# A planned two-headed kernel with its 64 planner draws exchanged

## The chip, the cores and the metric

The kernel runs on one core of one Trainium2 chip. The metric is the device time of one execution in microseconds (us); less is better. Five engines of the core matter here. PE (TensorE) multiplies matrices, with PEld as its weight load; ACT (ScalarE) does the exponentials; DVE (VectorE) and POOL (GpSimd) do element-wise work; SP (SyncE) issues most DMAs. Each engine takes its instructions strictly in the order of the program, and engines wait for one another by semaphores.

## The reference: what is computed

Two independent computations share the launch, and their results stand side by side in the output (2048 x 1280, bf16).

The first (A) is a diagonal complex state-space layer over 2048 steps and 640 states; the second (B) is attention with 32 query heads of width 20 that share one key head and one value head:

```python
# A
Bu = einsum("bld,pd->blp", x, B_bar)
h[t] = Lam_bar * h[t-1] + Bu[t]                 # complex, t = 0..2047
y = 2 * einsum("blp,dp->bld", hseq, Cmat).real + x * Dskip
# B
q, k, v = x @ wq (32 heads of 20), x @ wk, x @ wv
p = softmax(q k^T * 20**-0.5)                   # 32 x 2048 x 2048
out = (p v) @ wo
```

The bulk is the softmax: 32 heads x 2048 x 2048 exponentials.

## The kernel before, in words

**Attention.** The 2048 queries are cut in 4 blocks of 512, the 32 heads in 8 groups of 4 heads, which makes 32 groups; the keys are cut in 16 pieces of 128. A unit is one head, one query block and one key piece, 128 x 512 scores, so a group has 64 units and the program 2048. The loop of `main` takes a group's units in small sets. A set is a fill: PE computes two or three units at once into a PSUM tile (`R0` with three banks, `R1` with two, in turn), and ACT then takes the whole tile in one exponential, `ex_op` at L1295, 128x1024 or 128x1536 wide, into the SBUF tile `P`. One further unit can ride along with a fill: a D unit. Its scores go to one of two spare PSUM banks, `B`, or to the third bank of `R0`, which the fill then leaves to it and is two wide. A D unit gets its exponential on DVE instead of ACT: `dx_op` at L1301 turns the scores to an integer whose bits read as a bf16 power of two, and `sh_op` at L1307 makes three shifted copies, in two instructions for each run of one to four neighbouring units. Four copies of one unit take four product matmuls where an ACT unit takes one. PE then multiplies the results with the values `VP` into the PSUM bank `PV` (rows `PV<-P` and `PV<-Pd`), four column strips at a time. When a group's 64 units are in, DVE copies `PV` out (`OTr`, L1343), and only then can the next group's products begin. Later, normalising (POOL, L1039) and projection (PE rows with `WO`) follow.

**State-space layer.** Per block of 512 steps and per 128 states: PE products with `BTre` and `BTim`, a DVE rotation (L929), PE sums, two DVE scans (L957), 24 small POOL instructions (L945) and, once five such steps are through, output products with `CGre` and `CGim`, copied out at L990. All of it is put between the attention's instructions, as are the query projections (rows `B<-xbT,wq` and `B<-xbT,wqd`).

**What sets the order.** Nothing is written out by hand. `Plan` keeps a clock for each engine from its own table of costs. In each turn `main` offers all work that could go next, with the start that `Plan` gives it and a bias, and takes the lowest; that appends the instruction to its engine's program. The biases are not fixed: the 2048 units are cut in 64 turns of 32, and at the start of a turn `vary` seeds a random generator with that turn's entry of `SEEDS` and draws about twenty settings: how much DVE work may be queued before a unit is no longer sent to it (`backlog`), how long background work may starve, the largest number of D units of a group (`quota`), the biases of fills, products, copies, shifts (`pvb`, `rawb`, `shb`), how many D units share a shift (`shift`), and the size of a random term in every bias (`noise`). The core of it:

```python
if self.units * self.TURNS // NU > turn:
    turn = self.units * self.TURNS // NU
    self.vary(self.SEEDS[min(turn, self.TURNS - 1)])
```

One more rule matters: where `Plan` sees PE idle for longer than a limit and its recent work sparse, it puts in zero products (rows `PV<-cs,VP`), which add nothing to `PV`.

Until the first fill (the setup: transposed loads, the key projection, tables of sines) the order comes from code and not from draws.

Of the kernel before, what the change touches and what calls it, by code (L numbers as in the profile page):

```python
# [254 lines left out]
class _Kernel:  # L255
# [18 lines left out]


    TURNS = 64
    SEEDS = (31, 1860, 2783, 3329, 4215, 5944, 6425, 7348, 8334, 9235, 10124, 11344, 12674, 13859, 14008,
# [4 lines left out]

    def __init__(self, nc, t):
        self.nc, self.t = nc, t
# [874 lines left out]
    def main(self):  # L1159
# [188 lines left out]
        while True:  # L1348
# [3 lines that stand above are left out]
            cand = []  # L1352
# [216 lines left out]
```

## Time and profile before

| | before |
|---|---|
| median of 3 runs | 760.76 us (759.37 to 761.68) |
| profiled execution, own time | 759.82 us |
| its span, first to last instruction | 758.1 us |
| ACT busy | 743.4 us (98%) |
| DVE busy | 699.6 us (92%) |
| PE busy | 697.1 us (92%) |
| POOL busy | 347.5 us (46%) |

A row of the table of groups has the line, the engine, the operation, out<-in with the tiles' names, the shape and the count; behind the bar the busy time in us and the mean duration of one in ns, then the engine's idle time ahead of them with what ended it. Instructions of one engine overlap at their ends, so a group's busy time divided by its count is less than the mean duration of one. The chain that ended last follows the work back from the last instruction to what released it. PEclk is the clock granted to PE, 1.00 being full.

### The profile page before, as it was taken

The page shows a single profiled execution, that of the slowest core. Times are in us where ns is not written, and L with a number is a line of the kernel's source. Part 1 is how long each engine was busy: PE and PEld are TensorE (multiplying, and loading weights), DVE is VectorE, ACT ScalarE, POOL GpSimd, SP SyncE. Part 2 cuts the span into 40 slices and gives each one's busy share as a digit, 9 for nine tenths or more (in the row PEclk, how much of TensorE's full clock was granted, in tenths as well). Part 3 has the DMA queues.
Part 4 walks back from the last instruction along what each step waited for, and adds up shares of the span by engine and source line. Part 5 has one row for each costly group of instructions (what it writes and reads, how often), then busy time and mean ns, then how long its engine had stood idle before and what let it go on. Part 6 is the DMA issues. An engine that isn't in the chain of part 4 may idle for free.

```text
span 758.1 us, 22782 instructions
## 1 busy us (share of the span) xinstructions
PE 697.1 (92%) x9725; PEld 226.4 (30%) x9725; DVE 699.6 (92%) x1084; ACT 743.4 (98%) x705; POOL 347.5 (46%) x708
## 2 busy tenths in 40 slices
PE   5899988888899999999999999899999999998788
PEld 2322222222224333222343232233322233332224
DVE  6699999999997899999999799999999989999976
ACT  8999999999999999999999999999999999999996
POOL 5701455479887001998304975730068880000040
PEclk9799999999999999999999999999999999998999
DMA  9486301000002100400001310020100210010011
GB/s 187 73 131 146 67 16 49 18 15 16 2 24 63 42 28 21 87 17 16 18 27 49 70 42 24 9 59 11 33 24 11 59 38 31 24 33 9 11 44 36
DMA packets 61202, 31.89 MB, mean 42 GB/s; under 512 B 41510, under 2 KB 61102, under 8 KB 61102
## 3 DMA queue, kind: packets, MB, share of 16 engines
q1 hardware_dynamic: 59606, 30.14, 16.8%
q8 instruction: 77, 1.26, 0.7%
q10 hardware_dynamic: 1496, 0.30, 0.2%
q14 instruction: 23, 0.19, 0.1%
HBM read 9.21 MB, written 12.69 MB: 29 GB/s over the span
## 4 chain that ended last, share of the span: by engine, by line
ACT 87%; PE 9%; DVE 3%; DMA 1%; issue 0%; ACTq 0%
ACT P L1295 85%; PE R L448 3%; PE B L448 3%; PE PV L448 3%; DVE Pd L1301 1%; DVE Pd L1307 1%; ACT cs L719 1%; DMA WO<-in_B_wk_dram 1%; ACT Pd L718 0%; ACT KT L565 0%; ACT L530 0%; DVE hh L957 0%; DVE tm L929 0%; ACT WO L507 0%; ACTq L421 0%
## 5 line engine op out<-in xcount | busy, mean ns | idle before, releaser
L1295 ACT ACTIVATE P<-R 128x1024 bf16<-128x1024 f32 (+2 forms) x672 | 724.2, 1333 | 4.3 <-PE B L448 2.2
L448 PE MATMUL R<-QT,KT 32*128 32x512 bf16 (+1 forms) x1674 | 264.8, 388 | 46.2 <-ACT P L1295 36.3
L1301 DVE TENSOR_SCALAR Pd<-B 128x512 int16<-128x512 f32 x374 | 251.8, 682 | 22.1 <-PE B L448 19.6
L448 PE MATMUL PV<-Pd,VP 128*32 128x512 bf16 x1820 | 262.6, 386 | 1.4 <-DVE OTr L1343 0.5
L448 PE MATMUL PV<-P,VP 128*32 128x512 bf16 x1593 | 261.5, 386 | 0.2
L1307 DVE TENSOR_SCALAR Pd<-Pd 128x1536 int16<-128x1536 int16 (+3 forms) x342 | 241.0, 711 | 2.5
L945 POOL TENSOR_TENSOR tm<-hh,cs 128x128 bf16<-128x128 f32 x320 | 164.5, 538 | 31.4 <-DVE hh L957 17.2
L448 PEld LDWEIGHTS R<-QT,KT 32*128 32x128 bf16 (+1 forms) x1674 | 66.1, 91 | 307.4 <-ACT P L1295 279.7
L448 PE MATMUL B<-QT,KT 32*128 32x512 bf16 x374 | 144.5, 386 | 0.0
L945 POOL TENSOR_TENSOR W<-tm 128x128 bf16<-128x128 bf16 x160 | 76.0, 498 | 124.9 <-PE B L448 121.0
L1039 POOL TENSOR_TENSOR OTd<-OTd,rwide 128x128 bf16<-128x128 bf16 x80 | 34.0, 452 | 108.8 <-DMA OTd<-o_rows 106.9
L448 PEld LDWEIGHTS PV<-Pd,VP 128*32 128x32 bf16 x1820 | 63.1, 95 | 61.3 <-issue 41.0
L448 PEld LDWEIGHTS PV<-P,VP 128*32 128x32 bf16 x1593 | 62.3, 95 | 45.3 <-issue 36.1
L1301 DVE TENSOR_SCALAR Pd<-R 128x512 int16<-128x512 f32 x81 | 55.2, 682 | 2.7 <-PE R L448 1.9
L929 DVE TENSOR_TENSOR tm<-B,cs 128x1024 bf16<-128x1024 f32 x40 | 48.6, 1215 | 3.2 <-PE B L448 3.0
L448 PE MATMUL B<-CGre,W 128*32 128x384 bf16 (+1 forms) x640 | 48.5, 304 | 0.5 <-DVE Pd L1301 0.5
L448 PE MATMUL B<-CGim,W 128*32 128x384 bf16 (+1 forms) x640 | 47.8, 299 | 0.0
L886 POOL TENSOR_SCALAR tm<-W,sc 128x128 f32<-128x128 bf16 x40 | 32.7, 831 | 31.7 <-DVE CGre L888 14.9
L961 POOL COPY hst<-hh 128x2 f32<-128x2 f32 x15 | 5.9, 394 | 72.4 <-DVE hh L957 72.2
L957 DVE TENSOR_TENSOR_SCAN hh<-sc,hini,B 128x512 f32<-128x512 f32 x30 | 37.6, 1268 | 0.6 <-PE B L448 0.3
L448 PEld LDWEIGHTS B<-QT,KT 32*128 32x128 bf16 x374 | 33.9, 91 | 0.7 <-issue 0.4
L448 PE MATMUL B<-xaT,BTre 128*32 128x512 bf16 x400 | 30.8, 383 | 0.7 <-DVE hh L957 0.3
(153 smaller groups left out, 470.2 us busy)
## 6 DMA issues: line engine op xcount, KB each, us to landing
o_rows<-OTr SPq DMA_DIRECT2D x32, 128.0 KB, 1.7
QT<-q_rows SPq DMA_DIRECT2D x30, 128.0 KB, 2.2
q_rows<-Qd SPq DMA_DIRECT2D x16, 160.0 KB, 2.9
OTd<-o_rows SPq DMA_DIRECT2D x16, 160.0 KB, 3.3
out_dram<-ystage SPq DMA_DIRECT2D x16, 160.0 KB, 1.8
out_dram<-ostage SPq DMA_DIRECT2D x12, 160.0 KB, 1.8
P<-in_B_wq_dram SPq DMA_DIRECT2D x1, 800.0 KB, 6.1
WO<-in_B_wo_dram SPq DMA_DIRECT2D x4, 200.0 KB, 3.2
```

The source lines that it names most:

```text
L448: ins = e.matmul(o() if callable(o) else o, lhsT=l, rhs=r, start=st, stop=sp, skip_group_check=True, **kw)
L719: act(lambda e, c=c, b=b: e.activation(K.cs[:, c, :, :].rearrange("p i n -> p (i n)"), K.tri[:, 4 * b + 2:4 * b + 4, :].rearrange("p r n - ...
L886: pool(lambda e, y=y, c=c, gy=gy, i=i: e.tensor_scalar(K.ctmp[:, i:i + 128], y[:, i:i + 128], sc[:, gy, c:c + 1], None, op0=ALU.mult), key ...
L929: dve(lambda e, k=k, h=h: e.tensor_tensor(K.tm[:, 2 * k:2 * k + 2, :], bass.AP(tensor=K.BB, offset=512 * int(h.key[1]), ap=[[512 * self.BA ...
L945: put(lambda e, c0=c0, end=end: e.tensor_tensor(out[:, c0:end], a[:, c0:end], b[:, c0:end], op), reads, [writes + h], n, gate=None if i el ...
L957: dve(lambda e, ri=ri, ini=ini, h=h: e.tensor_tensor_scan(K.hh[:, ri, :], dec, h.T[:, :], ini, ALU.mult, ALU.add), ["sc", None, "hini"], [ ...
L961: pool(lambda e: e.tensor_copy(K.hst[:, :, c:c + 1], K.hh[:, :, 511:512]), ["hh0", "hh1"], ["hst"], 40)
L1039: ops.append(Op("pool", lambda e, c=c, m=m: e.tensor_tensor(K.OTd[:, m, c], K.OTd[:, m, c], K.rwide[:, c], ALU.mult), rw + [f"OTe{dd}" for ...
L1295: return Op("act", lambda e: e.activation(dst, K.R[n % 2][:, 0:512 * size], ACT.Exp, scale=self.exp_scale), [f"R{n % 2}"] + ["R0c"] * (siz ...
L1301: return Op("dve", lambda e: e.tensor_scalar(K.Pd[:, 0, u, :], K.B[x][:, :], self.d_off, 0.0, op0=ALU.add, op1=ALU.max), [key], [f"Pd{u}_0 ...
L1307: return Op("dve", lambda e: e.tensor_scalar(K.Pd[:, i:i + n, a:b, :].rearrange("p s u n -> p s (u n)"), K.Pd[:, 0:n, a:b, :].rearrange("p ...
```

## The change

All 64 entries of `SEEDS` are other numbers. No other line differs:

```diff
     TURNS = 64
-    SEEDS = (31, 1860, 2783, 3329, 4215, 5944, 6425, 7348, 8334, 9235, 10124, 11344, 12674, 13859, 14008,
...
+    SEEDS = (19, 1987, 2263, 3089, 4041, 5474, 6444, 7290, 8492, 9186, 10683, 11194, 12742, 13024, 14829,
...
```

So every turn draws other settings and another noise, and from the first draw on each engine's program stands in another order. The setup is the same, instruction for instruction. Counted over the whole program, these numbers differ:

| instructions | before | after |
|---|---|---|
| ACT exponentials 128x1536 / 128x1024 / 128x512 | 250 / 421 / 1 | 225 / 454 / 0 |
| D units, from `B` / from `R` | 374 / 81 | 362 / 103 |
| shift runs of 1 / 2 / 3 / 4 units | 27 / 32 / 84 / 28 | 37 / 35 / 66 / 40 |
| products `PV<-P` / `PV<-Pd` | 1593 / 1820 | 1583 / 1860 |
| zero products `PV<-cs,VP` | 212 | 100 |

Everything else has the same count on every engine.

The first place is PE's program right after the setup. `R<-QT,KT` are a fill's scores, `B<-QT,KT` a D unit's; `B<-xbT,wq` is the query projection for the second group, `B<-Qabs,Mblk` its last step, `B<-xbT,wqd` belongs to later groups. Before:

```order
L448 MATMUL R<-QT,KT 128x512 x7
L448 MATMUL B<-xbT,wq 32x512 x20
L448 MATMUL R<-QT,KT 128x512 x5
L448 MATMUL PV<-P,VP 32x512 x4
L448 MATMUL B<-Qabs,Mblk 32x512 x4
L448 MATMUL B<-xbT,wqd 32x512 x20
```

After:

```order
L448 MATMUL R<-QT,KT 128x512 x7
L448 MATMUL PV<-P,VP 32x512 x8
L448 MATMUL R<-QT,KT 128x512 x3
L448 MATMUL PV<-P,VP 32x512 x4
L448 MATMUL R<-QT,KT 128x512 x2
L448 MATMUL PV<-P,VP 32x512 x8
L448 MATMUL R<-QT,KT 128x512 x3
L448 MATMUL B<-QT,KT 128x512
L448 MATMUL B<-xbT,wq 32x512 x20
L448 MATMUL R<-QT,KT 128x512 x2
```

The 20 projection matmuls stood ahead of the ninth fill and now stand behind the eleventh; products of the first fills, in batches of 4 to 8, have their place.

The second place is PE's program where it has least to do for the longest. Before, at fills 616 to 619 of 672, some nine tenths through:

```order
L448 MATMUL R<-QT,KT 128x512 x2
L448 MATMUL B<-QT,KT 128x512
L448 MATMUL PV<-P,VP 32x512
L448 MATMUL PV<-Pd,VP 32x512 x5
L448 MATMUL R<-QT,KT 128x512 x3
L448 MATMUL B<-QT,KT 128x512
L448 MATMUL PV<-P,VP 32x512
L448 MATMUL R<-QT,KT 128x512 x2
L448 MATMUL B<-QT,KT 128x512
L448 MATMUL R<-QT,KT 128x512 x3
L448 MATMUL B<-QT,KT 128x512
L448 MATMUL PV<-Pd,VP 32x512 x2
```

After, at fills 620 to 622 of 679, the same share of the way through, where PE again has little beside its fills:

```order
L448 MATMUL R<-QT,KT 128x512 x2
L448 MATMUL B<-QT,KT 128x512
L448 MATMUL PV<-Pd,VP 32x512 x4
L448 MATMUL R<-QT,KT 128x512 x3
L448 MATMUL PV<-Pd,VP 32x512 x2
L448 MATMUL PV<-P,VP 32x512
L448 MATMUL PV<-Pd,VP 32x512 x3
L448 MATMUL R<-QT,KT 128x512 x2
L448 MATMUL B<-QT,KT 128x512
```

Before, one product and then none stood between three fills in a row; now four and six stand between neighbouring fills.

8 rows, old and new, of the table SEEDS are left out of this document.

## The prediction

> **What bounds the kernel now.** I read the page's busy times and chain first, then ACT's timeline, because the chain names ACT.
>
> ```profile
> PE 697.1 (92%) x9725; PEld 226.4 (30%) x9725; DVE 699.6 (92%) x1084; ACT 743.4 (98%) x705; POOL 347.5 (46%) x708
> ...
> ACT 87%; PE 9%; DVE 3%; DMA 1%; issue 0%; ACTq 0%
> ...
> L1295 ACT ACTIVATE P<-R 128x1024 bf16<-128x1024 f32 (+2 forms) x672 | 724.2, 1333 | 4.3 <-PE B L448 2.2
> ```
>
> The 672 exponentials occupy ACT for 724.2 us and ACT stood idle ahead of them for only 4.3 us. ACT's timeline in order of time has a new row wherever it had to wait (in brackets, with what ended the wait):
>
> ```profile
> 20.88 9.17 ACT L1295 ACTIVATE P<-R 128x1536 bf16<-128x1536 f32 x8
> 31.30 2.37 ACT L1295 ACTIVATE P<-R 128x1536 bf16<-128x1536 f32 x2 [1.25 <-PE R L448]
> 34.27 196.33 ACT L1295 ACTIVATE P<-R 128x1536 bf16<-128x1536 f32 x178 [0.60 <-PE B L448]
> 230.93 115.15 ACT L1295 ACTIVATE P<-R 128x1536 bf16<-128x1536 f32 x108 [0.33 <-PE B L448]
> 346.46 345.61 ACT L1295 ACTIVATE P<-R 128x1536 bf16<-128x1536 f32 x326 [0.38 <-PE R L448]
> 693.08 2.53 ACT L1295 ACTIVATE P<-R 128x1536 bf16<-128x1536 f32 x2 [1.01 <-PE B L448]
> 695.87 53.49 ACT L1295 ACTIVATE P<-R 128x1536 bf16<-128x1536 f32 x48 [0.26 <-PE B L448]
> 753.52 0.70 ACT L1129 ACTIVATE W<-R 128x640 bf16<-128x640 f32 x1 [4.15 <-PE R L448]
> ```
>
> So the span is 20.88 us of setup, 724 us of exponentials, some 4 us of waits among them, and 758.1 - 749.36 = 8.7 us of tail. A wait on ACT costs its full length; on any other engine it costs nothing until ACT waits. DVE and PE are not idle partners, though:
>
> ```profile
> 40.00:740.00 700.00, 652.43 (x9132) 208.12 (x9133) 662.70 (x1010) 697.60 (x650) 321.34 (x643) 1.00 0.15 37
> 60.00:160.00 100.00, 86.32 (x1066) 24.12 (x1058) 97.51 (x155) 100.00 (x91) 44.84 (x61) 1.00 0.23 53
> 640.00:688.00 48.00, 45.61 (x715) 15.94 (x712) 47.27 (x80) 48.00 (x48) 0.00 (x0) 1.00 0.09 30
> ```
>
> These rows of busy time by stage (length, then PE, PEld, DVE, ACT, POOL, clock) show DVE at 662.70 / 700 = 94.7% in the middle of the program, and at 97.5% and 98.5% in stretches in which ACT still never waited.
>
> **The change, part by part.** *ACT's work.* 25 exponentials of 1536, and one of 512, become 33 of 1024, since ten more units go to DVE. Their price is the pace in an unbroken run, from two runs of the timeline split by form:
>
> ```profile
> L1295 ACT ACTIVATE P<-R 128x1536 bf16<-128x1536 f32 x76 | 124.3, 1635 | 0.7 <-PE B L448 0.6
> L1295 ACT ACTIVATE P<-R 128x1024 bf16<-128x1024 f32 x102 | 116.2, 1187 | 0.1
> ...
> L1295 ACT ACTIVATE P<-R 128x1024 bf16<-128x1024 f32 x218 | 227.9, 1177 | 0.0
> L1295 ACT ACTIVATE P<-R 128x1536 bf16<-128x1536 f32 x108 | 172.3, 1595 | 0.5 <-PE R L448 0.4
> ```
>
> With 76 b + 102 a = 196.33 and 108 b + 218 a = 345.61, a 1024 takes a = 0.912 us and a 1536 takes b = 1.360. Over the program 421 a + 250 b is 723.9, which with one of 512 meets the 724.2 of the page. The change is 33 x 0.912 - 25 x 1.360 - 0.46 (half a 1024) = **-4.4 us**. This is sure, being counts; what may be lost is the filling of ACT.
>
> *The start.* ACT's waits of 1.25 and 0.60 us come from here (the chain):
>
> ```profile
> 21.04 6.77 ACT P L1295 x6
> 27.85 0.61 PE R L448 x2
> 28.46 2.26 PE B L448 x20
> 30.72 1.08 PE R L448 x5
> 31.80 0.55 PE PV L448 x4
> 32.35 1.54 PE B L448 x24
> ```
>
> The ninth fill stands behind 20 projection matmuls, 2.26 us, and ACT, through with its eighth tile at 20.88 + 9.17 = 30.05, waits. After, eight products stand there, at 0.55 a batch of four about 1.1 us, so that fill begins near 29.6 and is there by 30.1. Two further fills (0.54 each) and 12 products (1.65) end near 32.9, with the ninth and tenth exponential over at about 32.4: 0.5 us lost. Then the 20 projections come; at the later pace (a batch of 24 in 1.54 us) about 1.2 us, and the fill behind them is there by 34.5 with ACT's eleventh over at about 34.2: 0.3 lost. At the earlier pace it would be 1.1 us more. The batch also feeds the second group's queries later, which delays D units, not ACT. Of 1.85 us 0.8 stay: **-1.0**, between -1.8 and +0.1.
>
> *The fall of the clock near 688 us.* Waits of 1.01 and 0.26 us come from this stretch (columns as above):
>
> ```profile
> 684.00:688.00 4.00, 2.82 (x29) 0.79 (x24) 4.00 (x7) 4.00 (x5) 0.00 (x0) 1.00 0.11 37
> 688.00:692.00 4.00, 3.50 (x31) 0.82 (x30) 3.97 (x6) 4.00 (x4) 0.00 (x0) 0.51 0.00 0
> 692.00:696.00 4.00, 4.00 (x43) 0.82 (x35) 2.49 (x5) 2.67 (x4) 0.00 (x0) 0.64 0.00 0
> ```
>
> PE had 2.82 us of work in 4, its clock was then 0.51, and work that had fitted no longer did. In PE's order this is the sparsest place of the program: fills 617 to 620 have 9 matmuls of other work among them (counted from the order). The next is 10, at fill 635, and there the timeline shows no wait. After the change the smallest such sum over four fills is 14 (at fills 470 and 620), and PE has fewer holes although zero products are halved. I take this fall as gone, **-1.3**; bounds -1.3 (no fall) and +1.3 (it recurs at two places).
>
> ```profile
> 686.69 0.39 PE L448 MATMUL R<-QT,KT 32*128 32x512 bf16 x3 [0.95 <-ACT P L1295]
> ```
>
> By the Trainium skill, page "TensorE: Matmul & The Clock Gate", section "What's actually happening", the clock drops after an idle window of some 3.4 us and stays up without such gaps. PE's longest wait in that stretch is the 0.95 us of the row above, so a window that is busy to two thirds suffices here; taken at its word the rule would see a fall in neither kernel, this term would be chance, and the sum 1.3 us higher.
>
> *DVE's work.* Ten more D units and another mix of shift runs:
>
> ```profile
> L1301 DVE TENSOR_SCALAR Pd<-B 128x512 int16<-128x512 f32 x374 | 251.8, 682 | 22.1 <-PE B L448 19.6
> L1307 DVE TENSOR_SCALAR Pd<-Pd 128x3072 int16<-128x3072 int16 x84 | 81.8, 974 | 0.5
> ...
> L1307 DVE TENSOR_SCALAR Pd<-Pd 128x1536 int16<-128x1536 int16 x84 | 48.0, 572 | 0.5
> L1307 DVE TENSOR_SCALAR Pd<-Pd 128x2048 int16<-128x2048 int16 x60 | 43.5, 725 | 0.7
> ...
> L1307 DVE TENSOR_SCALAR Pd<-Pd 128x4096 int16<-128x4096 int16 x28 | 35.4, 1264 | 0.1
> L1307 DVE TENSOR_SCALAR Pd<-Pd 128x1024 int16<-128x1024 int16 x59 | 25.9, 445 | 0.7
> ...
> L1307 DVE TENSOR_SCALAR Pd<-Pd 128x512 int16<-128x512 int16 x27 | 8.0, 297 | 0.1
> ```
>
> Ten at 251.8 / 374 are 6.7 us. A run of one, two, three, four units costs 0.74, 1.17, 1.55, 1.99 us (both its instructions), so +10, +3, -18, +12 of them are 7.4 + 3.5 - 27.9 + 23.9 = 6.9. Together 13.6 us more on DVE, in a middle stretch some 6 us shorter: (662.7 + 13.6) / 694 = 97.4%. That is what it reached for 100 us at a time without a wait of ACT, but now for 694. While DVE keeps up this lies wholly beside ACT. I take **+1.5** for waits that it will cause somewhere, four times the 0.38 us wait at 346 us; bounds 0 and 9.8 (DVE's idle time in the middle, 37.3 us, falls only half of the way to the 17.7 that are left).
>
> ```profile
> L945 POOL TENSOR_TENSOR tm<-hh,cs 128x128 bf16<-128x128 f32 x320 | 164.5, 538 | 31.4 <-DVE hh L957 17.2
> ```
>
> The Trainium skill, page "SBUF — State Buffer", section "Who interferes with whom", calls the port pair of DVE's fast modes and POOL an exclusive lock, whose loser blocks for the whole instruction. The 14 added shift instructions could by that block for a POOL piece each, an estimate of 14 x 0.54 = 7.5 us by the row above, all on DVE; by it DVE's middle share would be (676.3 + 7.5) / 694 = 98.5%, and the durations that I used already hold what contention there was.
>
> ```profile
> L448 PE MATMUL PV<-cs,VP 128*32 128x512 bf16 x212 | 18.2, 382 | 0.0
> ...
> L945 POOL TENSOR_TENSOR W<-tm 128x128 bf16<-128x128 bf16 x160 | 76.0, 498 | 124.9 <-PE B L448 121.0
> ```
>
> ```profile
> 728.96 9.17 POOL L1039 TENSOR_TENSOR OTd<-OTd,rwide 128x128 bf16<-128x128 bf16 x20 [104.75 <-DMA OTd<-o_rows]
> ```
>
> *PE's work.* Seven more fills (two tiles in 0.61 us at the start: 4.3) and 30 more products (at the zero products' pace of 18.2 / 212: 2.6) are 7 us at most, and 112 zero products fewer take off 9.6. PE has 47.6 us free in the middle stretch; 0. *POOL's work* is the same but late: the last sums that it waits for stand at fill 610 of 679, before at 537 of 672. Its 24 pieces a step take 8.2 + 3.8 = 12.0 us by the two `L945` rows, and the first output product that needs them stands 16 fills on, some 17 us at 724.2 / 672 each; covered, and POOL was idle for 104.75 us there before; 0. If that cover goes, PE stands at fill 626 with every later fill behind it. *The tail* has the same list of instructions but for two groups of products behind the last fill, under the wait for the last exponential; 0.
>
> The sum against the profiled execution's own time (its span of 758.1 and 1.7 around it): 759.8 - 4.4 - 1.0 - 1.3 + 1.5 = 754.6. The median of the runs stood 0.9 us above that execution, so I forecast 755.5 us, 0.7% faster.
>
> **Rivals.** *The filling is given back.* DVE or PE make ACT wait for 6.5 to 11 us in all instead of the 3.5 that my terms leave (4.3 - 1.0 - 1.3 + 1.5): 758.5 to 763. For it: DVE at 97.4% with 17.7 us in reserve, and orders drawn at random need not fall as well as those of before, with 4.3 us lost in 724. Against it: PE loses 5 us of work, and DVE's peaks of 98.5% cost nothing.
>
> *DVE becomes the bound (the other side).* If DVE can't be filled better than the 94.7% that it had, its 676.3 us take 714 instead of 700, and the time is 760.8 + 14 = 775. It decides from the share at which the middle lasts 702.3 us and the time passes 763: 96.3%. For it: D units wait for two or three banks that background work also uses, and DVE did stand idle 22.1 us for `PE B`. Against it: 97.5% over 100 us.
>
> *The clock falls at all sparse places.* Five places of the new order have 16 or fewer matmuls among four fills. At 1.3 to 1.9 us each (the two losses of before) that is 6 to 9 us on 755.5: 762 to 765. Against it: before has the sum 10 at fill 635 and loses nothing.
>
> **Chances.** My forecast 0.64, its own range 751.9 (760.8 - 4.4 - 1.8 - 1.3 + 0 = 753.3, less the 1.4 us that the lowest run lies under the median) to 758.4; given back 0.20; DVE the bound 0.10; clock 0.06, split at 763. About 0.3%, 2.3 us, is what a measurement of this kernel can tell from no change. So faster 0.64, within it 0.20 + 0.03 = 0.23, slower 0.13. The range takes in the forecast's and the first rival's, 751.9 to 763.0, and leaves out DVE as the bound and half of the clock's case.
>
> **What the next profile would show.** ACT's exponentials busy 720 us; idle ahead of them near 3.5 us, with no long first wait at 31 us and no clock below 1.00 after 40 us; DVE's middle share near 97%. I am wrong if the idle time ahead of the exponentials passes 6.5 us, and then the engine that ended most of it says which rival it was.

## The result, and the profile after

| | before | after |
|---|---|---|
| median | 760.49 us (759.37 to 762.53, 8 runs) | 756.98 us (755.55 to 758.68, 8 runs) |
| profiled execution, own time | 759.82 us | 756.86 us |
| its span | 758.1 us | 755.1 us |
| first exponential begins | 20.88 us | 21.08 us |
| first exponential to the end of the last | 728.48 us | 724.78 us |
| tail behind it | 8.73 us | 9.26 us |

The ratio is 0.9951, with a 95% interval of 0.9935 to 0.9967: 0.5% faster. A second comparison (`after_again` below) gave 0.9943 [0.9925, 0.9961].

The page of after: busy times, the shares of the chain that ended last, and the exponentials.

```profile
PE 699.2 (93%) x9643; PEld 225.0 (30%) x9643; DVE 711.0 (94%) x1108; ACT 740.4 (98%) x712; POOL 349.3 (46%) x708
...
ACT 63%; PE 21%; DVE 14%; issue 1%; POOL 1%; ACTq 0%; DVEq 0%
...
L1295 ACT ACTIVATE P<-R 128x1024 bf16<-128x1024 f32 (+1 forms) x679 | 721.0, 1296 | 3.7 <-PE R L448 1.7
```

In the exponentials ACT is busy for 3.2 us less (724.2 before), and ahead of them idle for 0.6 us less. DVE has 11.4 us more work. ACT's share of the chain fell from 87% to 63%: over a third of the span PE and DVE now finish just when ACT needs them. That looks like a change of bound, but the idle time of 3.7 us says that ACT hardly waits for them.

ACT's timeline of after, in the columns of the prediction:

```profile
21.08 11.51 ACT L1295 ACTIVATE P<-R 128x1536 bf16<-128x1536 f32 x10
32.84 1.45 ACT L1295 ACTIVATE P<-R 128x1536 bf16<-128x1536 f32 x1 [0.25 <-PE B L448]
34.76 20.09 ACT L1295 ACTIVATE P<-R 128x1024 bf16<-128x1024 f32 x19 [0.46 <-PE B L448]
55.01 277.24 ACT L1295 ACTIVATE P<-R 128x1536 bf16<-128x1536 f32 x259 [0.16 <-PE B L448]
332.41 29.43 ACT L1295 ACTIVATE P<-R 128x1024 bf16<-128x1024 f32 x28 [0.17 <-PE B L448]
362.16 8.17 ACT L1295 ACTIVATE P<-R 128x1024 bf16<-128x1024 f32 x7 [0.32 <-PE B L448]
371.42 144.55 ACT L1295 ACTIVATE P<-R 128x1536 bf16<-128x1536 f32 x138 [1.09 <-PE R L448]
516.56 229.30 ACT L1295 ACTIVATE P<-R 128x1024 bf16<-128x1024 f32 x217 [0.60 <-PE R L448]
```

The waits at the start are 0.25 + 0.46 = 0.71 us, where before had 1.85. From 516 us to the end ACT does not stop once, so the old waits near 693 us are gone. But there is a new one of 1.09 us at 371 us. Busy time by stage around it (PE, PEld, DVE, ACT, POOL, clock, DMA), the middle of the program first:

```profile
40.00:740.00 700.00, 658.78 (x9132) 208.50 (x9124) 678.16 (x1040) 696.98 (x658) 323.15 (x643) 1.00 0.15 37
...
360.00:364.00 4.00, 3.50 (x44) 0.92 (x36) 4.00 (x7) 3.68 (x5) 3.84 (x9) 1.00 0.00 0
364.00:368.00 4.00, 3.30 (x26) 0.71 (x26) 3.96 (x7) 3.88 (x5) 3.76 (x10) 0.58 0.21 66
368.00:372.00 4.00, 4.00 (x37) 0.89 (x33) 3.24 (x5) 2.91 (x3) 2.11 (x4) 0.56 0.02 4
...
361.30:364.70 3.40, 2.20 (x26) 0.63 (x22) 3.40 (x7) 3.08 (x4) 3.17 (x8) 1.00 0.00 0
118.90:122.30 3.40, 2.25 (x27) 0.62 (x27) 3.37 (x6) 3.40 (x5) 0.63 (x1) 1.00 0.45 110
```

DVE's middle share is 678.16 / 700 = 96.9%. And the clock fell again, from 364.7 to 371.5 us, at fills 318 to 321, a place that the prediction did not name.

**When the clock falls.** The clock's changes of both traces lie on a grid. Before it rose at 32.7 us and fell at 688.1, 192.0 times 3.413 us later; after it rose at 33.6 and fell at 364.7, 97.0 times that later. A fall lasts one or two steps of the grid (3.4 or 6.8 us), the cold start usually three. In the step ahead of its fall PE was busy for 2.20 / 3.40 = 65% in after (the row of 361.30 above) and for 66% in before:

```profile
684.70:688.10 3.40, 2.26 (x23) 0.69 (x23) 3.40 (x6) 3.40 (x4) 0.00 (x0) 1.00 0.13 43
```

At 118.90, with 66%, after did not fall. Over the traces of before, after and the twelve experiments I counted all 2859 steps at full clock between 34 and 745 us: of 18 in which PE was busy to less than 0.64, 16 were followed by a fall; of 38 between 0.64 and 0.69, 13; of 2803 above 0.69, none. (Busy is meant as the profile has it; the ends of matmuls are modelled.) The grid's place against the program differs from run to run: the cold start ended between 30.6 and 35.7 us in the 14 traces. So a place that is sparse for 3 or 4 us falls in some runs, when one step lies wholly in it, and in others not. This is the free-running window of 3413 ns of the Trainium skill, page "TensorE: Matmul & The Clock Gate", section "What's actually happening", and the grid agrees with it. What it says of an idle window does not: here a window busy to two thirds was enough in 13 of 38 cases.

**What a fall costs.** Each run has its mean clock. With the cold start alone it is 0.993; each step at half clock takes some 0.0023 off. The 14 runs of the changed kernel in the two comparisons, sorted by it:

| mean clock | steps at half clock beyond the start's three | times, us |
|---|---|---|
| 0.993 | 0 | 755.37, 755.44 |
| 0.991 | 1 | 755.58, 756.05, 756.31, 757.94 |
| 0.988, 0.989 | 2 | 755.55, 755.88, 756.76, 756.86, 757.10 |
| 0.986 | 3 | 757.47, 757.95 |
| 0.984 | 4 | 758.68 |

From none to four the time rises by 3.3 us, 0.8 us a step; a straight line through all 14 gives 0.7. Without a fall the kernel takes 755.4 us, by two runs. The middle column is an estimate: the mean clock also counts a fall in the tail (after has one, from 753.8 us on) and would count a longer cold start, though the traces of this order have three steps there. It is a relation between runs and not a price of each fall: in the traces ACT's waits behind one fall run from none (`after_again` at 120.9 us) to 1.27 us (before at 688, two waits). And in before's own 52 later runs the time does not follow the mean clock: the six at 0.993 took 759.99 to 761.18 us, amid the others. (The cold start of before's order takes two to four steps in its traces, which blurs this.)

### The profile page after: what moved, and what is told of

It is laid out like the page before. It is cut to its first block, busy times and chain, and to the rows that moved or that the text cites. A ratio compares the mean times of both kernels' runs of the same rounds, so it can differ in the third digit from the quotient of the medians.

```text
span 755.1 us, 22636 instructions
## 1 busy us (share of the span) xinstructions
PE 699.2 (93%) x9643; PEld 225.0 (30%) x9643; DVE 711.0 (94%) x1108; ACT 740.4 (98%) x712; POOL 349.3 (46%) x708
## 4 chain that ended last, share of the span: by engine, by line
ACT 63%; PE 21%; DVE 14%; issue 1%; POOL 1%; ACTq 0%; DVEq 0%
ACT P L1295 61%; PE R L448 7%; PE PV L448 7%; PE B L448 7%; DVE Pd L1307 5%; DVE Pd L1301 5%; DVE hh L957 2%; DVE tm L929 1%; ACT cs L719 0%; ACT KT L565 0%; DVE ostage L1089 0%; DVE OTr L1343 0%; ACT Pd L718 0%; DVE Qd L803 0%; ACTq L421 0%
## 5 line engine op out<-in xcount | busy, mean ns | idle before, releaser
L1295 ACT ACTIVATE P<-R 128x1024 bf16<-128x1024 f32 (+1 forms) x679 | 721.0, 1296 | 3.7 <-PE R L448 1.7
L448 PE MATMUL PV<-Pd,VP 128*32 128x512 bf16 x1860 | 271.2, 385 | 4.0 <-DVE Pd L1307 1.7
L448 PE MATMUL PV<-P,VP 128*32 128x512 bf16 x1583 | 265.5, 389 | 0.4
L1301 DVE TENSOR_SCALAR Pd<-B 128x512 int16<-128x512 f32 x362 | 243.8, 681 | 15.4 <-PE B L448 13.1
L1307 DVE TENSOR_SCALAR Pd<-Pd 128x1536 int16<-128x1536 int16 (+3 forms) x356 | 250.0, 709 | 2.8
L945 POOL TENSOR_TENSOR tm<-hh,cs 128x128 bf16<-128x128 f32 x320 | 161.1, 528 | 162.9 <-DVE hh L957 153.5
L448 PE MATMUL B<-QT,KT 32*128 32x512 bf16 x362 | 140.0, 387 | 0.0
L945 POOL TENSOR_TENSOR W<-tm 128x128 bf16<-128x128 bf16 x160 | 79.9, 523 | 37.2 <-PE B L448 33.0
L1301 DVE TENSOR_SCALAR Pd<-R 128x512 int16<-128x512 f32 x103 | 69.9, 678 | 1.3 <-PE R L448 1.0
L448 PE MATMUL B<-xaT,BTim 128*32 128x512 bf16 x400 | 32.3, 395 | 0.5 <-DVE tm L929 0.2
```

The lines of the kernel that those rows point to most:

```text
L448: ins = e.matmul(o() if callable(o) else o, lhsT=l, rhs=r, start=st, stop=sp, skip_group_check=True, **kw)
L945: put(lambda e, c0=c0, end=end: e.tensor_tensor(out[:, c0:end], a[:, c0:end], b[:, c0:end], op), reads, [writes + h], n, gate=None if i el ...
L1295: return Op("act", lambda e: e.activation(dst, K.R[n % 2][:, 0:512 * size], ACT.Exp, scale=self.exp_scale), [f"R{n % 2}"] + ["R0c"] * (siz ...
L1301: return Op("dve", lambda e: e.tensor_scalar(K.Pd[:, 0, u, :], K.B[x][:, :], self.d_off, 0.0, op0=ALU.add, op1=ALU.max), [key], [f"Pd{u}_0 ...
L1307: return Op("dve", lambda e: e.tensor_scalar(K.Pd[:, i:i + n, a:b, :].rearrange("p s u n -> p s (u n)"), K.Pd[:, 0:n, a:b, :].rearrange("p ...
```

## The experiments

All ratios are to runs of before taken together with the version, with 95% intervals. "ACT's work" is the sum of the exponentials at 0.904 us (1024 wide) and 1.330 us (1536), the shortest steps from start to start of neighbours, which are the same in both traces; "excess" is the stretch from the first exponential to the last less that work. Before has 713.5 us of work and 14.9 of excess, after 709.7 and 15.1.

**Filling the sparse place of after.** The scores of two fills are issued more often than needed, so that PE is busy there. The edit in `fill_op`, here for fills 318 and 319 counted from 0:

```diff
-            return self.mms(lst, sorted(reads), writes, kind="QK")
+            o = self.mms(lst, sorted(reads), writes, kind="QK")
+            again = {318: 1, 319: 3}.get(n, 0) if out else 0
+            if again:
+                one = o.fn
+
+                def fn(e):
+                    for _ in range(again):
+                        one(e)
+                    return one(e)
+                o.fn = fn
+            return o
```

> The kernel after, with the score products of two fills computed more often: fill 319 (three units wide, at 362.5 us) twice, fill 320 (at 363.6 us) four times; same order, same data. In the kernel after the clock was 0.5 from 364.7 to 371.5 us and ACT waited 1.09 us behind it; the stretch of 3.41 us that ended at 364.7 had PE busy for 66% of it, the least of all such stretches counted from 33.6 us. Theory (the clock falls at the end of a fixed stretch of 3.41 us in which PE was busy for less than about two thirds): the stretch is now busy for more than 75%, no fall near 365 us, the wait of 1.09 us is gone and that place costs about 1.1 us less; in the runs' median some 0.5 us, since the stretches lie elsewhere in other runs. Rival (the fall has another cause, such as the wait of 0.73 us for DVE in that place): the clock falls there all the same.

Measured: 755.4 us (755.13 to 756.53), ratio 0.9921 [0.9896, 0.9945]. Busy time by stage, and ACT's timeline from 332 us on:

```profile
364.00:368.00 4.00, 3.14 (x37) 0.75 (x29) 4.00 (x8) 3.93 (x5) 3.77 (x9) 1.00 0.23 70
368.00:372.00 4.00, 4.00 (x60) 1.21 (x57) 4.00 (x5) 4.00 (x4) 1.85 (x4) 1.00 0.00 0
```

```profile
332.34 182.13 ACT L1305 ACTIVATE P<-R 128x1024 bf16<-128x1024 f32 x173 [0.16 <-PE B L448]
515.06 97.55 ACT L1305 ACTIVATE P<-R 128x1024 bf16<-128x1024 f32 x94 [0.60 <-PE R L448]
```

The clock stays at 1.00, and ACT runs through from 332.34 to 514.47. The grid lay at the same place in both executions (the cold start ended at 33.57 us in after and at 33.53 here), so the step that had 65% in after can be put beside the same one here. It has 3.27 / 3.40 = 96%:

```profile
361.20:364.60 3.40, 3.27 (x45) 0.91 (x37) 3.40 (x7) 3.29 (x4) 3.17 (x8) 1.00 0.00 0
```

The wait of 1.09 us at 371 is gone with the fall, as it is in `after_again` below, the same program without a fall there: that the fall caused it is shown. The wait of 0.32 us at 362, ahead of the fall, went here too; why is open. The whole stretch of exponentials is 1.5 us shorter than in after.

**The same in before**, with `{617: 3, 618: 1, 619: 1}`:

> The kernel before, with the score products of three fills computed more often: fill 618 (at 685.4 us) four times, 619 and 620 twice. In the kernel before the clock was 0.5 from 688.1 to 694.9 us with waits of ACT of 1.01 and 0.26 us; the stretch of 3.41 us that ended at 688.1 had PE busy for 66%, the least of all. Theory (as above): no fall there, waits of 1.3 us gone, 0 to 1.3 us faster by the median (0.0 to 0.17%). Rival: the clock falls there all the same, no change.

Measured: 761.12 us, ratio 0.9991 [0.9972, 1.001], no gain that can be told from nothing. The fall at 688 us was gone, but the profiled execution fell at the second sparsest place, fill 635, which had shown none in before:

```profile
706.50:709.90 3.40, 2.09 (x20) 0.50 (x17) 3.31 (x6) 3.40 (x4) 0.00 (x0) 1.00 0.11 39
709.90:716.80 6.90, 6.83 (x53) 1.38 (x53) 5.02 (x9) 5.66 (x6) 0.00 (x0) 0.51 0.04 7
```

PE was busy to 2.09 / 3.40 = 61% in a step of the grid there. So a fall that one trace does not show may stand in the next.

**All sparse places of after**, in the same way: `{85: 1, 87: 2, 89: 2, 107: 1, 108: 1, 123: 1, 124: 1, 318: 1, 319: 3, 661: 2, 663: 2}`, and beside it **after itself**.

> The order of after, with the score matmuls of eleven fills issued one to three times more than needed (same operands, same PSUM banks, so the scores are the same): at fills 85, 87, 89, 107, 108, 123, 124, 318, 319, 661 and 663, counted from 0, all places of the program where PE has least to do. Nothing else differs. Theory (at a sparse place the clock falls if a window of 3.4 us there is busy to less than about two thirds, and which place it hits differs from run to run, because the windows lie elsewhere): no run falls after the start, so the time is that of after_more_scores, 755.4 us, or up to 0.5 less, a ratio to before of 0.991 to 0.993, 1.0 to 1.6 us under after_again in the same call. Rival (the added matmuls hold up other fills, or the gain of after_more_scores was the lie of the windows in its runs): no faster than after_again.

> The changed kernel itself, for comparison on the same chip in the same call. 757.0 us, ratio to before 0.995, with one fall of the clock after the start in its profile at one of the sparse places (fills 86 to 88, 107 to 108, 123, 318 to 321, 661 to 663), or none.

Measured: 755.71 us (754.86 to 757.20), ratio 0.9935 [0.9916, 0.9954], against 756.18 us (755.37 to 757.95), 0.9943 [0.9925, 0.9961], for after again. Five of the six runs with added scores had a mean clock of 0.993 or more, that is no fall, and two of the six runs of after. The 0.5 us between the medians, where 1.0 to 1.6 were expected, is less than either interval is wide: whether the added scores make the kernel faster in general is not settled. The version is not worse, and no version here beats after by what can be measured.

Its profiled execution took 757.20 us without any fall. PE's timeline shows why:

```profile
69.64 0.39 PE L448 MATMUL R<-QT,KT 32*128 32x512 bf16 x2 [1.49 <-DMA QT<-q_rows]
```

The fill waited 1.49 us for queries of the next group, which make a round trip through DRAM, and ACT then 1.37 us for the fill. In after the same matmuls did not wait; in `after_again` they waited 0.68 us. The load was issued at 64.8 us in after, at 66.1 in `after_again` and at 65.5 here, where the fill began only 4.1 us later. So when a load comes is a second thing that differs from run to run, by its issue and by its way, with at least 1.4 us in it.

**Without zero products.** Each batch of zero products becomes one matmul of a single column, 25 batches in after and 53 in before:

```diff
-                    self.go(self.mms([self.m1(K.PV[:, :], zeros, K.cs[:, 0, 0, :], False, False)],
-                                     ["VP", "cosT"], ["PV"], accum=True, kind="zero"))
...
+                    z.fn = lambda e: e.matmul(K.PV[0:32, 0:1], lhsT=zeros[:, 0:32],
+                                              rhs=K.cs[:, 0, 0, 0:1], start=False, stop=False, skip_group_check=True,
+                                              tile_position=(0, 0))
...
```

> The kernel after, with each group of four zero products of 512 columns shrunk to one of a single column; 25 groups, about 0.22 us of PE work each, taken away, order unchanged. Theory (stretches of 3.41 us under two thirds busy): counted over all positions of the stretches in the trace of after, 1.0 stretches on average are under 66% with the zero products and 3.2 without, so about two more falls at 1.2 us, 2.7 us slower than after (ratio to before about 0.9985). Rival (zero products only fill holes): within 0.5 us of after.

> The kernel before, with its 53 groups of zero products shrunk in the same way. Theory: in the trace of before 1.9 stretches on average are under 66% with the zero products and 10.5 without, so about nine more falls at 1.2 us, some 10 us slower (ratio 1.013). Rival: within 0.5 us of before.

Measured: after 757.1 us, ratio 0.9944 [0.9918, 0.997]; before 766.98 us, 1.0077 [1.0051, 1.0103]. The exponentials of the two, after first:

```profile
L1295 ACT ACTIVATE P<-R 128x1024 bf16<-128x1024 f32 (+1 forms) x679 | 721.3, 1285 | 4.2 <-PE B L448 1.9 <-PE R L448 1.6
```

```profile
L1295 ACT ACTIVATE P<-R 128x1024 bf16<-128x1024 f32 (+2 forms) x672 | 725.7, 1304 | 15.2 <-PE R L448 7.6 <-PE B L448 6.1 <-PE PV L448 1.0
```

After falls at three places then (119, 368 and 675 us, four steps in all), and loses nothing that can be measured: its ratio is that of after (0.9951 and 0.9943), its idle time 4.2 us against 3.7. For after the rival was right. Before loses 5.9 us (761.11 for its runs beside these). It falls at six places in its profiled execution (773.03 us, the slowest of its ten), beginning at 56 us, and its idle time rises from 4.3 to 15.2. So before's order needs its zero products; that after's needs its own, half as many, is not shown. Both expectations were too high. For after the falls came and cost next to nothing. For before the mean clock of the runs (median 0.975 against 0.989) stands for some six more steps at half clock, not nine more falls, at about 1 us each.

**More work on DVE, by memsets.** A memset of one column ahead of every D unit's conversion, 59 ns each by rows of the setup:

```diff
+            def fn(e):
+                e.memset(K.spare[:, u:u + 1], 0.0)
+                return e.tensor_scalar(K.Pd[:, 0, u, :], K.B[x][:, :], self.d_off, 0.0, op0=ALU.add, op1=ALU.max)
...
```

> The kernel after, with a DVE memset of one element per partition (the setup's smallest memsets take 59 to 61 ns) ahead of each of the 465 D units' first instruction, on a spare tile: about 28 us more DVE work, nothing else. DVE was idle for 21.8 us of the 700 between 40 and 740 us. Forecast's theory (ACT sets the pace, DVE has a reserve): the reserve is overdrawn by 6 us, so at least 6 and about 10 us slower than after (ratio to before about 1.008). Rival (DVE is off the path): within 1 us of after. Second rival (DVE is already the bound): the full 28 us slower.

> The kernel before, with the same memset ahead of each of its 455 D units: about 27 us more DVE work. DVE was idle for 37.3 us of the 700 between 40 and 740 us. Forecast's theory: the reserve holds it, 2 to 6 us slower (ratio about 1.005), clearly less than what the same does to after. Rival (DVE is off the path): within 1 us. Second rival (each us on DVE counts): the full 27 us.

Measured: after 757.46 us, 0.9952 [0.9937, 0.9967], no loss; before 764.48, 1.0031 [1.0009, 1.0054]. After's groups and its middle:

```profile
L1304 DVE MEMSET spare<- 128x1 f32 x465 | 27.4, 59 | 0.0
```

```profile
40.00:740.00 700.00, 657.55 (x9120) 208.73 (x9116) 680.93 (x1497) 696.78 (x658) 320.81 (x643) 1.00 0.15 37
```

27.4 us of memsets raised DVE's busy time in the middle by 680.93 - 678.16 = 2.8 us. They lie under the neighbouring instructions, so this did not load DVE and tells nothing of its reserve. Why before lost 0.3% all the same is open. Its profiled execution, 5.2 us longer than before's, shows where half of that went:

```profile
54.29 0.61 PE L449 MATMUL B<-xaT,BTre 128*32 128x512 bf16 x8 [2.66 <-issue]
```

Here PE stood 2.66 us ahead of the first state-space product, and ACT 2.58 us for the fill behind it. In the trace of before:

```profile
52.27 0.61 PE L448 MATMUL B<-xaT,BTre 128*32 128x512 bf16 x8 [0.22 <-issue]
```

The profile names no releaser. The last of the five `BTre` loads that this product reads was issued at 50.5 us here and at 49.0 in before, and these loads landed 2.9 to 4.7 us after their issue; that the wait is for them is argued from those times and was not tried. The memsets are not its cause: `before_more_scores`, which is before instruction for instruction up to this place, has the same wait of PE with 1.48 us, and ACT one of 1.39 behind it; `before_dve_reads` and `before_no_zeros` have 2.28 and 1.63 us, and ACT 2.19 behind each. So of five traces of before's order the one that the prediction was made from is the only one nearly without it. In the order of after this product stands later, at 53.5 to 54.1 us in all seven of its traces, with 0.35 us of wait at most. So this is likely a gain of the change that neither the forecast nor the two profiled executions hold; how much it adds to the medians was not measured.

**More work on DVE, by reads of PSUM.** Ahead of every second D unit DVE copies 8 columns of the same bank:

```diff
+            def fn(e):
+                if n % 2:
+                    e.tensor_copy(K.spare[:, u, :], K.B[x][:, 0:8])
+                return e.tensor_scalar(K.Pd[:, 0, u, :], K.B[x][:, :], self.d_off, 0.0, op0=ALU.add, op1=ALU.max)
...
```

> The order of after; ahead of every second D unit's conversion DVE copies 8 columns of the same PSUM bank into a spare tile, about 232 instructions of an estimated 170 ns (a copy of 128x10 in the setup took 168), some 75 of them inside the overlap of neighbouring ends, so about 0.095 us each, 22 us more on DVE, against 21.8 us that DVE stood idle between 40 and 740 us in after and 37.3 in before. The memsets of after_dve_more did not load DVE; this is their repetition with a read of PSUM, which the profile's middle share has to show. Theory (DVE can be filled to about 97.5% over the whole middle, no further): 678.2 + 22 = 700 us need 718, so after loses about 20 us, 777. Rival (DVE has no cap but its own work, and waits only move): 700 us of work fit in 700, the loss is 2 to 6 us, 759 to 763.

> The order of before with the same copies, about 228. Theory (cap at 97.5%): 662.7 + 22 = 684.7 us of 700, 97.8%, so before loses 2 to 5 us, a ratio of 1.003 to 1.007, much less than after loses. Rival (the units are late by what stands ahead of each, not by the sum): both lose the same.

Measured: after 763.28 us, 1.0039 [1.0023, 1.0055], which is 7.1 us above after again; before 767.43 us, 1.009 [1.0067, 1.0113], 7.4 us above before. The middle and the exponentials of after, then the middle of before:

```profile
40.00:740.00 700.00, 653.70 (x9008) 207.58 (x9003) 683.14 (x1255) 692.14 (x651) 318.62 (x637) 0.99 0.15 37
...
L1296 ACT ACTIVATE P<-R 128x1024 bf16<-128x1024 f32 (+1 forms) x679 | 724.2, 1233 | 8.1 <-PE B L449 4.1 <-PE R L449 2.9
```

```profile
40.00:740.00 700.00, 649.87 (x9005) 205.87 (x9001) 669.46 (x1223) 691.67 (x641) 313.95 (x629) 0.99 0.15 38
```

The copies added 11 to 12 us of busy time to DVE (722.9 against 711.8 in after again, 712.0 against 699.6), half of what I had reckoned. Both orders lost the same, though after's DVE stands at 97.6% and before's at 95.6%. After alone would not speak against a cap: 678.2 + 11.5 us at 97.5% take 707 us, about the 7 us that it lost. It is before that does: 662.7 + 12 us are 96.4% of 700, so by the cap it should have lost nothing. Of the two rivals the one that said that both lose the same was right; the other had 2 to 6 us for after and fell short by one. That the cost is single D units that come late, because the order did not know of the copies, fits this but is argued. The change itself put 11.4 us more on DVE, in an order made with that work in it, and lost next to nothing (excess 14.9 to 15.1 us).

**Parts of the draws.** The first 48 entries of after's `SEEDS` with the last 16 of before's, and 64 random numbers, of which this is the first line:

```diff
-    SEEDS = (19, 1987, 2263, 3089, 4041, 5474, 6444, 7290, 8492, 9186, 10683, 11194, 12742, 13024, 14829,
+    SEEDS = (140891, 596853, 888598, 841235,
...
```

> The entries of SEEDS are those of after for the first 48 turns and those of before for the last 16. Its program has 236 exponentials of 1536 and 443 of 1024: at the shortest steps between starts that both traces show, 1.330 and 0.904 us, that is 714.4 us of ACT work, 0.9 more than before (713.5) and 4.7 more than after (709.7). Theory (ACT's work sets the time between orders, with waits as in after): 4.7 us above after, about 761.7. Rival (the gain of after lies in the better filled first three quarters, the start above all): about 757 to 759.

> 64 entries drawn at random, not searched. Its program has 260 exponentials of 1536 and 423 of 1024: 728.2 us of ACT work at the same steps, 14.7 more than before; 422 D units. Theory (ACT's work sets the time): 760.5 + 14.7 = 775 us (ratio 1.019), with waits of 4 to 8 us ahead of the exponentials. Rival (orders differ as much by their holes as by their ACT work): 780 us or more, with waits of over 10 us.

Measured: 761.43 us, 1.0002 [0.9986, 1.0018], and 783.34 us, 1.028 [1.0245, 1.0316]. The first came out as the theory had it (761.7). It has 714.4 us of ACT's work and 13.5 us of excess: its waits are as few as after's, its start is after's, and still it takes as long as before, as its work does. The random draws:

```profile
L1291 ACT ACTIVATE P<-R 128x1024 bf16<-128x1024 f32 (+1 forms) x683 | 740.8, 1302 | 12.2 <-PE B L444 5.3 <-PE R L444 3.3 <-PE PV L444 2.7
```

728.2 us of ACT's work, 24.4 us of excess and seven falls of the clock. ACT's work alone would have given 775 us; the rival was right here, with 780 us or more and over 10 us of waits. Of the 24.8 us that they lie above before in span, 14.7 are work and 9.4 excess. The time of an order is the work that it leaves to ACT plus what is lost in filling ACT; after differs from before mainly by the first.

## Why the prediction was right, and where not

The forecast was 755.5 us and 0.7% faster; it came out at 756.98 and 0.5%. Sign, range and the main term held. Between the profiled executions the sum had -5.2 us, and they show -3.0. The medians came closer to the forecast than that by luck: the 0.9 us added for the distance from the profiled execution to the median turned out as 0.1 (756.86 and 756.98). The terms:

| term | predicted | in the traces |
|---|---|---|
| ACT's work | -4.4 | -3.9 |
| the start | -1.0 | -1.1 |
| the fall of the clock | -1.3 | -0.2 |
| new waits | +1.5 | +0.5 |
| delays too short for a row of the timeline | not listed | +1.0 |
| first exponential, and tail | 0 | +0.2 and +0.5 |

The delays are what is left: the excess rose by 0.2 us, while the waits in the rows fell by 0.8.

*ACT's work.* Right in kind and sure as a count; the prices were too far apart. Solving two runs of the timeline gave 0.912 and 1.360 us, but the runs that they were solved from hold delays too short to see. The shortest steps are 0.904 and 1.330: 33 x 0.904 - 25 x 1.330 - 0.46 = -3.9.

*The start.* Two waits went and two smaller ones came, 0.71 us for the predicted 0.8.

*The fall of the clock: the step that failed.* "I take this fall as gone" was right for the place and wrong for the program. The count of other matmuls over four fills picked fills 470 and 620 as the sparsest of the new order; the fall came at 318 to 321. A step of the grid is shorter than four fills, and what counts is PE's busy time within it. Worse, it was priced as a property of the order, gone or there, when it is a chance that each run draws: by their mean clocks some 12 of 14 runs of the changed kernel had a fall somewhere, and before, in another execution, fell elsewhere (`before_more_scores`). The bounds of that term, -1.3 to +1.3, did hold it. Without a fall the kernel takes 755.4 us; that this is the forecast to 0.1 us is chance, since ACT's work was 0.5 too large and delays of 1.0 us were not in the sum. Of the signs named beforehand this is the one that failed ("no clock below 1.00 after 40 us"); 720 us of exponentials, 3.5 us of idle time and 97% for DVE came out as 721.0, 3.7 and 96.9. The rival "the clock falls at all sparse places" priced a fall at 1.3 to 1.9 us; the runs say 0.7 to 0.8 us a step, and 758.7 us in the one with four.

*New waits from DVE.* +0.5 for +1.5, the waits at 55, 332, 362 and 516 us less those of 0.33 and 0.38 us that before had. With the short delays it is the +1.5 that was forecast, but nothing shows that all of them are DVE's, so the agreement may be luck. DVE did not become the bound: its middle share passed the 96.3% that would decide, to 96.9%, near the 97.4% of the sum and not the 98.5% of the estimate with blocking. The idle time of 3.7 us was near the forecast's 3.5, and so "the filling is given back" is out too.

*PE, POOL.* Zero held: from 516 us on ACT does not wait, and the late sums of POOL are there. But PE did not lose work. The first rival's "PE loses 5 us of work" does not follow from the terms above it, which give 9.6 - 7 = 2.6, and PE's busy time in the middle rose by 6.4 us (652.43 to 658.78).

*Tail and first exponential.* Both had zero. The tail was between 8.7 and 9.1 us in the six later traces of this order, and the first exponential began between 20.9 and 21.6 us in all traces but one, so these 0.7 us belong to the execution and not to the change.

## What to carry to other kernels

Where one engine bounds and the others are planned around it, price a new order first by the work that it leaves to that engine, at the shortest step between neighbours and not at the mean of a run, and take the waits from the filling of comparable orders. A wait that stands in one trace is a draw: clock falls and late loads come and go from run to run, so a term for one that goes away should hold its chance, and the chance that the next sparsest place takes it over. Spare percentages of a second engine say little; work that the order was made with cost nothing here at 97%, and the same amount put in behind its back cost 7 us at 96% as well.

## What the runs showed of the hardware

- PE's clock halves behind a window of 3.413 us in which PE was busy to less than some two thirds (16 of 18 below 0.64, 13 of 38 up to 0.69, none above), on a grid that is fixed within an execution and mostly lies elsewhere in the next; the longest single wait of PE ahead of before's fall was under 1 us. A fall lasts one or two windows; in the order of after a run is 0.7 to 0.8 us longer for each window.
- Two steps at 0.56 and 0.57 were not followed by a fall. One is the step with the late queries at 67.4 us:

```profile
67.40:70.80 3.40, 1.91 (x26) 0.56 (x30) 2.68 (x6) 2.03 (x3) 2.66 (x4) 1.00 0.97 93
```

  Both have a single wait of about 1.5 us in them, where the windows that fell at 0.50 to 0.64 have two to four, none over 0.9 us but one of 1.27. Yet three windows with a single wait of 2.0 to 2.3 us, busy to 0.33 to 0.41, did fall. What the gate counts beside busy time stays open.
- A memset of 59 ns ahead of an instruction that reads PSUM costs DVE almost nothing (2.8 us for some 460 in the middle), a copy of 8 columns out of PSUM, 157 ns, about a third of its duration (11 us for 232).
